# Two attention batches get their transposed queries from the DMA crossbar, and the hand-written step order is set anew

## The chip, the cores and the metric

The kernel runs on one core of a Trainium2 chip. The metric is the device time of one execution in microseconds (us). The kernel before took 223.79 us, the median of 5 runs (223.52 to 224.37).

## What is computed

The program is an attention with 32 memory slots per head, followed by a channel mix over the whole model width. There are 8 batches, 8 heads, 576 tokens per batch, head size 64, model width 512 and inner width 1024.

```python
a = exp(phi - max(phi, axis=2)); a = a / (sum(a, axis=2) + 1e-09)      # over the tokens
k_m = einsum('bhsm,bhsd->bhmd', a, k);  v_m = einsum('bhsm,bhsd->bhmd', a, v)
attn = softmax(scale * q @ k_m^T);  x = attn @ v_m                     # [B, S, H*D] after a transpose
x_prev = x shifted by one token
xk = mu_k * x + (1 - mu_k) * x_prev;  xr = mu_r * x + (1 - mu_r) * x_prev
out = sigmoid(xr @ w_r) * (relu(xk @ w_k) ** 2 @ w_v)
```

## The kernel before, in words

**Two halves, one order.** The channel mix walks over 9 chunks (c0 to c8) of 512 tokens. A chunk is 16 groups of matmuls: eight "key" groups (`key`, L510: four 128x512 matmuls, a ReLU on ScalarE and a square on VectorE), four "gate" groups (`gate`, L526) and four "value" groups (`value`, L543, which ends in a product on VectorE and in stores on SyncE's queue). The attention of a batch is some 30 small steps (`attention`, L234). A step and a chunk group both have a number, their slot: the groups have slots 0 to 143, and a step of batch b has the position in its table plus 16 times (b - 1), or the bare position for batch 0. The program sorts everything by slot and emits it (L562 to L572). So the tables decide in which order each engine gets its instructions; each engine then runs its own list in order, and waits only on data and on buffers. A step whose position is lower stands earlier in the queues of all engines that it uses.

**The tables.** `STEADY` (L18) holds the order for every batch without a table of its own. `FIRST` (L23) has tables for batches 0 to 3 before. Letters behind a `+` are the PSUM buffers that the step takes in turn: `a` is a pool of three banks that only attention uses, `k` the two banks of the key groups, `v` the three banks that gates and values use. Without letters a step takes `a`.

**The steps that matter here.** `exp` (L246) exponentiates phi on ScalarE. `kv`, or `k` and `v` apart (L254), are 40 small matmuls. `z` (L270) is the sum and its reciprocal on VectorE. `nk` (L279) scales k on VectorE, `tk` (L302) transposes it on TensorE and copies it out on VectorE. `q0` to `q3` (L320) transpose the queries: six 96x96 transposes on TensorE and one 128x576 copy on VectorE each. `s0` and `s1` (L331) are the scores and their exponentials on ScalarE; they read all four query pieces between them. `l0` to `l3` (L348) are the denominators with a logarithm on ScalarE, `r..z` and `h..z` (L360) the reciprocals on ScalarE, `w` and `y` (L365) the products on VectorE. For batches 2 to 7, `nv`, `x0` to `x3` (L372), `dd` (L389) and `k0d`, `k2d`, `r0d`, `r2d` (L401) make the values, the shifted difference and the mix. Batches 0 and 1 take another way: `nkx` and `nrx` (L411) put mu into the values (eight VectorE operations), and `mk0` to `mr3` (L428) are the mixed values by matmul, each copied out half by ScalarE, half by VectorE. `mub` (L212) loads mu into `mu_b` by four DMAs on SyncE's queue, `mum` (L226) multiplies it out on VectorE, and `busy` (L205) puts matmuls of zeros on TensorE: 18 in all before.

**Queries and loads.** `load` (L298) of batch b issues the loads of batch b + 2 on GpSimd's queue. Query tiles `qs` and transposed query tiles `qT` have two buffers each, so a batch follows the batch two before it into the same buffer. A step `qx` (`cross_q`, L316) is there but in no table before: it makes the whole `qT` of a batch with one transposing DMA on SyncE's queue:

```python
nc.sync.dma_start_transpose(out=q_tile().rearrange("p h j t -> p (h j) t"),
                            in_=qs[b % 2].rearrange("p h j d -> p (h j d)"))
```

Of the kernel before, what the change touches and what calls it, by code (L numbers as in the profile page):

```python
# [14 lines left out]

STEADY = [("exp", -20), ("q3", -16), ("q2", -15), ("kv+v", -14), ("z+v", -12), ("nk", -12), ("nv", -12),  # L18
          ("q1", -11), ("q0", -11), ("tk+v", -11), ("s1+aa", -8), ("s0+va", -8), ("load", -7),
          ("l1+a", -6), ("l0+k", -6), ("l3+a", -6), ("r0z", -6), ("w0", -4), ("l2+a", -1), ("r1z",  # L20
          0), ("w1", 0), ("x0+av", 2), ("x3+aa", 4), ("x2+vv", 6), ("x1+aa", 6), ("dd", 8), ("r0d",
          9), ("k2d", 12), ("k0d", 13), ("r2d", 22)]
FIRST = {  # L23
    0: [("busy2_748059", -69), ("busy1_148982", -61), ("busy2_192243", -58), ("exp", -58), ("mub", -55),
        ("mu", -51), ("k+a", -50), ("z+v", -50), ("nk", -47), ("busy1_9643", -46), ("mum", -43),
        ("tk+k", -43), ("q0", -42), ("q1+v", -42), ("q3+a", -41), ("q2+v", -35), ("s0+av", -33),
        ("l0+v", -31), ("l1+a", -31), ("s1+va", -25), ("h0z", -25), ("y0", -23), ("h1z", -23),
        ("busy3_339813", -20), ("l2+k", -19), ("l3+v", -18), ("busy3_529042", -18), ("v+v", -15),
        ("y1", -15), ("h2z", -13), ("nkx", -12), ("busy2_337394", -11), ("busy1_474373", -10),
        ("y2", -9), ("h3z", -9), ("load+a", -7), ("y3", -6), ("mk0+kk", -6), ("mk1+a", -6),  # L30
        ("busy1_380911", -5), ("mk2+aa", -5), ("mk3+vv", -3), ("busy1_810794", -2), ("nrx", -2),
        ("mr1+aa", 2), ("mr2+vv", 4), ("busy1_47294", 4), ("mr0+vv", 4), ("mr3+aa", 4)],
    1: [("exp", 5), ("z+v", 7), ("k+a", 8), ("q0+v", 9), ("q2", 9), ("nk", 9), ("q3", 9), ("q1+v", 9),
        ("tk+v", 10), ("s0+aa", 10), ("s1+va", 10), ("l1+a", 11), ("l3", 11), ("l0+v", 11), ("h3z",
        11), ("h0z", 11), ("l2+k", 11), ("h1z", 11), ("v+k", 12), ("nkx", 12), ("nrx", 12), ("y0",
        12), ("y3", 12), ("y1", 12), ("h2z", 14), ("y2", 14), ("mk0+kv", 14), ("mr1+va", 14),
        ("mk3+vv", 14), ("mr3+kk", 14), ("mk2+aa", 14), ("mk1+vv", 15), ("mr0+ka", 15), ("load+a",
        16), ("mr2+av", 17)],
    2: [("exp", -4), ("q0", -1), ("q1+v", -1), ("q3+a", 0), ("z+k", 0), ("kv+v", 0), ("nk", 0), ("tk+v",
        1), ("q2", 1), ("s0+kv", 2), ("s1+va", 2), ("l0+v", 3), ("l1+a", 3), ("load+k", 3), ("r0z",  # L40
        4), ("w0", 5), ("nv", 5), ("l3+a", 5), ("l2+v", 5), ("r1z", 6), ("x0+a", 8), ("w1", 9),
# [4 lines left out]
        ("l3+k", 5), ("r0z", 5), ("w0", 5), ("r1z", 5), ("w1", 6), ("x0+ka", 7), ("x1+va", 7),  # L46
        ("x2+vv", 8), ("x3+kk", 8), ("dd", 9), ("k2d", 9), ("load+k", 9), ("k0d", 11), ("r2d", 13),
        ("r0d", 15)],
}
LOADS = {None: ("phi", "k", "v", "q"), 2: ("phi", "k", "q", "v"), 3: ("phi", "k", "q", "v"), 4: ("phi", "k", "q", "v")}  # L50
ORDER = ('phi', 'k', 'q', 'wv', 'v')
# [11 lines left out]
def kernel(  # L63
# [13 lines left out]
    nc = tc.nc  # L77
# [145 lines left out]
        nc.tensor.transpose(ps_mu, mu2, ident_f)  # L223
        nc.vector.tensor_scalar_add(mu1, ps_mu, -1.0)

    def spread_mu():  # L226

        for w in range(2):
            mask = maskk.rearrange("p h d -> p (h d)").unsqueeze(1).to_broadcast([128, 2, 2 * D])
            nc.vector.tensor_mul(mu_m[:, w, 0], mask, mu_b[:, w])  # L230
            nc.vector.tensor_sub(mu_m[:, w, 1], mask, mu_m[:, w, 0])


    def attention(b):  # L234
        st = {}

        def ps_tile(shape, dtype, name):

            tags = st["tags"]
            tag = {"a": "at", "k": "pk", "v": "pv"}[tags[st["n"] % len(tags)]]  # L240
            st["n"] += 1
            return psum.tile(shape, dtype, name=name, tag=tag, bufs={"at": 3, "pk": 2, "pv": 3}[tag])
        x0 = b * S % RING
# [10 lines left out]
        def ekv(parts):  # L254

            def go():
                w = parts.stop - parts.start
                kvps = ps_tile([128, 2, w, D], F32, "kvps")
                for i in range(w):
                    st["kv"[parts.start + i]] = kvps[:, :, i, :]  # L260
                for j in range(NJ):
                    for h in range(H):
                        c, g = divmod(h, 4)
                        nc.tensor.matmul(kvps[g * M:(g + 1) * M, c], lhsT=em[:, j, h, :],  # L264
                                         rhs=kv5[:, parts, h, j, :],
                                         start=j == 0 and c == 0, stop=j == NB,
                                         skip_group_check=True)
            return go
# [42 lines left out]
        def q_tile():  # L311
            if "qT" not in st:
                st["qT"] = work.tile([128, H, NQ // 2, QR], BF16, name="qT", tag="qT")
            return st["qT"]
# [5 lines left out]
        def tr_q(pr):  # L320
            def go():
                ps = ps_tile([128, 2, NQ // 2, QR], BF16, "qtps")
                for i in range(2):
                    for j in range(NQ // 2):
                        nc.tensor.matmul(ps[:, i, j], rhs=identity[:QR, :QR], is_transpose=True,  # L325
                                         lhsT=qs[b % 2][:, 2 * pr + i, 2 * j:2 * j + 2, :].rearrange("p j d -> p (j d)"),
                                         start=True, stop=True, skip_group_check=True)
                nc.vector.tensor_copy(q_tile()[:, 2 * pr:2 * pr + 2], ps)  # L328
            return go

        def scores(c):  # L331
# [96 lines left out]
        def mixed(w, c, hf):  # L428

            def go():  # L430
# [15 lines left out]
                for jj in range(2):  # L446
# [3 lines left out]

        two = [(0, 0), (0, 1), (1, 0), (1, 1)]
        steps = {"exp": exp_phi, "kv": ekv(slice(0, 2)), "k": ekv(slice(0, 1)), "v": ekv(slice(1, 2)),
                 "z": esum, "nk": norm_k, "nv": norm_v, "tk": tr_k, "load": reload, "mu": load_mu, "mub": load_mu_b, "mum": spread_mu, "qx": cross_q}
        for i in range(4):
            steps[f"q{i}"] = tr_q(i)
            steps[f"l{i}"] = denom(*two[i])
# [106 lines left out]
    for b in range(B):  # L563
        steps = attention(b)
        for n, (name, pos) in enumerate(FIRST[b] if b in FIRST else STEADY):
            todo.append((pos + 16 * (b - 1) if b > 0 else pos, b, n, steps(name)))
# [36 lines left out]
```

## Time and profile before

| | us |
|---|---|
| median of 5 runs | 223.79 |
| the profiled execution, its own time | 224.37 |
| its span, first to last instruction | 222.6 |
| TensorE matmul busy | 206.5 (93%) |
| ScalarE busy | 159.7 (72%) |
| VectorE busy | 142.6 (64%) |
| query transposes on TensorE (192) | 12.4 |
| query copies on VectorE (32) | 13.4 |
| matmuls of zeros (18) | 8.3 |

The time of an execution is longer than the span by what lies before the first and after the last instruction, here 1.77 us. TensorE's busy time counts each matmul from its start to its modelled end, and matmuls overlap: the chain of waits, which counts each stretch of time once, shows what a group really adds. "PEld" is the weight load that precedes a matmul. SyncE's queue ("SPq") carries the stores, and an instruction in it can start only when those ahead of it have been issued.

### The profile page before, as it was taken

To read this page: it belongs to the slowest core of one execution; us is meant where nothing else is said; L and a number is where in the kernel's file an instruction comes from. 1 tells how busy PE (TensorE), PEld (TensorE's weight loads), DVE (VectorE), ACT (ScalarE), POOL (GpSimd) and SP (SyncE) were. 2 spreads that over 40 slices of the span, in tenths; PEclk is the share of its full clock that TensorE was granted. 3 is DMA by queue.
4 is the path that set the end of the run, shared out by engine and by line. 5 is a ranking of instruction groups with operands and counts; after the bars stand their busy time and mean duration, and the time that the engine had idled before them with its cause. 6 is when DMAs were issued, how large, how long until landed. Compare 5 with 4: busy or idle time off the path is not lost.

```text
span 222.6 us, 4576 instructions
## 1 busy us (share of the span) xinstructions
PE 206.5 (93%) x1755; PEld 101.8 (46%) x1755; DVE 142.6 (64%) x356; ACT 159.7 (72%) x309; POOL 47.7 (21%) x66
## 2 busy tenths in 40 slices
PE   4369999899999998999999999999999999999992
PEld 1243345346444564445444864454443444444441
DVE  3162855297565989788867688769875875425322
ACT  2207468983799849997699679967978965765770
POOL 7653351543340639121600000000000000000000
PEclk9999999999999999999999999999999999999998
DMA  6999999999999999999994300330033033033024
GB/s 135 194 200 207 231 204 209 222 222 275 218 238 197 262 202 210 231 197 307 144 187 111 94 3 0 94 97 1 10 98 85 1 94 94 3 94 94 0 65 124
DMA packets 43349, 31.49 MB, mean 141 GB/s; under 512 B 10952, under 2 KB 37840, under 8 KB 43328
## 3 DMA queue, kind: packets, MB, share of 16 engines
q0 software_dynamic: 35248, 20.91, 63.3%
q1 hardware_dynamic: 7776, 9.97, 15.7%
q10 hardware_dynamic: 304, 0.33, 0.4%
q8 instruction: 13, 0.21, 0.4%
q14 instruction: 8, 0.07, 0.1%
HBM read 38.54 MB, written 9.44 MB: 216 GB/s over the span
## 4 chain that ended last, share of the span: by engine, by line
PE 82%; DVE 5%; ACT 4%; DMA 3%; POOL 1%; issue 1%; SPq 1%; DVEq 0%; POOLq 0%
PE pk L518 28%; PE pv L551 27%; PE pr L532 13%; DMA mu_b<-in_moe_mu_r_dram 3%; PE qtps L325 2%; PE kvps L264 2%; PE idle L209 2%; PE nops L382 2%; PE zps L355 2%; PE scps L341 1%; DVE atn L369 1%; PE mxps L439 1%; DVE o L553 1%; ACT e L345 1%; PE zps L274 1%
## 5 line engine op out<-in xcount | busy, mean ns | idle before, releaser
L518 PE MATMUL pk<-xkT,wk 128*128 128x512 bf16 (+1 forms) x320 | 69.4, 358 | 0.0
L551 PE MATMUL pv<-wv,sq 128*128 128x512 bf16 (+1 forms) x296 | 66.2, 373 | 0.0
L522 ACT ACTIVATE rl<-pk 128x512 bf16<-128x512 f32 x72 | 43.1, 601 | 27.0 <-PE pk L518 26.7
L523 DVE TENSOR_TENSOR sq<-rl 128x512 bf16<-128x512 bf16 x72 | 30.4, 422 | 26.0 <-ACT rl L522 25.5
L553 DVE TENSOR_TENSOR o<-sg,pv 128x512 f32<-128x512 f32 (+1 forms) x37 | 24.2, 672 | 31.3 <-ACT sg L540 18.3
L551 PEld LDWEIGHTS <-sq 128*128 128x128 bf16 x296 | 28.6, 98 | 32.0 <-issue 0.4
L518 PEld LDWEIGHTS <-wk 128*128 128x128 bf16 x320 | 29.0, 98 | 26.2 <-issue 1.6
L532 PE MATMUL pr<-wr,xrT 128*128 128x512 bf16 x144 | 35.1, 379 | 0.0
L537 ACT ACTIVATE sg<-pr 128x512 f32<-128x512 f32 x36 | 21.6, 604 | 6.8 <-PE pr L532 6.5
L532 PEld LDWEIGHTS <-xrT 128*128 128x128 bf16 x144 | 13.3, 98 | 15.9 <-issue 1.2
L540 ACT ACTIVATE sg<-sg 128x1024 f32<-128x1024 f32 x18 | 19.0, 1057 | 0.6
L539 ACT ACTIVATE sg<-sg 128x1024 f32<-128x1024 f32 x18 | 19.0, 1057 | 0.6
L345 ACT ACTIVATE e<-scps 128x288 bf16<-128x288 f32 x32 | 10.8, 428 | 9.9 <-PE scps L341 9.9
L407 DVE TENSOR_SCALAR mu_d<-diff,mu 128x576 bf16<-128x576 bf16 x48 | 16.3, 382 | 0.2
L386 ACT CAST x<-nops 128x288 bf16<-128x288 f32 x48 | 16.0, 416 | 0.0
L328 DVE COPY qT<-qtps 128x576 bf16<-128x576 bf16 x32 | 13.4, 448 | 1.3 <-PE qtps L325 1.3
L369 DVE TENSOR_TENSOR atn<-e,lz 128x576 bf16<-128x576 bf16 (+1 forms) x20 | 12.3, 632 | 2.9 <-ACT lz L362 2.5
L325 PE MATMUL qtps<-identity,q 96*128 96x96 bf16 x192 | 12.4, 215 | 0.8 <-DMA q<-in_q_dram 0.8
L325 PEld LDWEIGHTS <-q 96*128 96x128 bf16 x192 | 10.9, 103 | 4.3 <-DMA q<-in_q_dram 1.2
L357 ACT ACTIVATE lz<-zps 128x288 f32<-128x288 f32 x32 | 11.2, 411 | 1.2 <-PE zps L355 1.2
L362 ACT ACTIVATE lz<-lz 128x576 f32<-128x576 f32 (+1 forms) x20 | 11.4, 596 | 0.0
L248 ACT ACTIVATE em<-phm 128x1024 bf16<-128x1024 f32 x8 | 8.4, 1055 | 3.3 <-DMA phm<-in_phi_dram 3.3
(66 smaller groups left out, 188.0 us busy)
## 6 DMA issues: line engine op xcount, KB each, us to landing
out_dram<-o SPq DMA_DIRECT2D x23, 192.0 KB, 2.3
kv<-in_k_dram POOLq DMA_DIRECT2D x8, 512.0 KB, 12.3
q<-in_q_dram POOLq DMA_DIRECT2D x7, 576.0 KB, 15.1
phm<-in_phi_dram POOLq DMA_DIRECT2D x7, 512.0 KB, 13.1
kv<-in_v_dram POOLq DMA_DIRECT2D x7, 512.0 KB, 13.4
out_dram<-o SPq DMA_DIRECT2D x23, 128.0 KB, 2.4
out_dram<-o SPq DMA_DIRECT2D x23, 64.0 KB, 2.0
wk<-in_moe_w_k_dram POOLq DMA_DIRECT2D x2, 512.0 KB, 12.3
```

Source lines behind the costliest of these rows:

```text
L325: nc.tensor.matmul(ps[:, i, j], rhs=identity[:QR, :QR], is_transpose=True, lhsT=qs[b % 2][:, 2 * pr + i, 2 * j:2 * j + 2, :].rearrange("p ...
L386: nc.scalar.copy(st["x"][:, 2 * c + jj, sl], pss[jj])
L407: nc.vector.tensor_scalar_mul(t[:, i], st["d"][:, pr + i, :], mu1[:, o:o + 1])
L518: nc.tensor.matmul(pk[:, lo:hi], lhsT=wk_sb[:, di, fi * 128:(fi + 1) * 128], rhs=xk_T[:, di, c0:c0 + hi - lo], start=(di == 0), stop=(di = ...
L522: nc.scalar.activation(rl, pk, AF.Relu)
L523: nc.vector.tensor_mul(st["sq"][:, fi, :], rl, rl)
L532: nc.tensor.matmul(pr, lhsT=xr_T[:, di, c0:c0 + 128], rhs=wr_sb[:, di, :], start=(di == 0), stop=(di == ND - 1))
L537: nc.scalar.activation(sg[:, ts % 2], pr, AF.Exp, scale=-1.0)
L539: nc.scalar.activation(sg, sg, AF.Ln, bias=1.0)
L540: nc.scalar.activation(sg, sg, AF.Exp, scale=-1.0)
L551: nc.tensor.matmul(pv[:, cols], lhsT=st["sq"][:, fi, ts * 128:(ts + 1) * 128], rhs=wv_sb[:, fi, cols], start=(fi == 0), stop=(fi == NF - 1))
L553: nc.vector.tensor_mul(o[:, cols], st[ts // 2][:, ts % 2, cols], pv[:, cols])
```

## The change

Batches 6 and 7 get tables of their own. In them `q0` to `q3` are gone and one `qx` stands in their place, at slot 59 for batch 6 (position -21) and at slot 88 for batch 7 (position -8); the scores of the two batches stand at slots 71 and 88. `STEADY` is then used by batches 4 and 5 only, and its steps move by up to three slots, with `q1`, `q3` and `x3` on other buffers. The tables of batches 0 and 1 are new: for batch 0 the matmuls of zeros go from 18 to 9, `mum` is cut in two (`mum0` for mu_k, `mum1` for mu_r), `z` goes ahead of `mub` and `k`, and the copies of `q1` and `q3` go from VectorE to ScalarE; for batch 1 the steps `y0` to `nrx` move to slots 12 and 13 and all eight `m` steps to slot 15. Tables 2 and 3 are the same.

```diff
-STEADY = [("exp", -20), ("q3", -16), ("q2", -15), ("kv+v", -14), ("z+v", -12), ("nk", -12), ("nv", -12),
-          ("q1", -11), ("q0", -11), ("tk+v", -11), ("s1+aa", -8), ("s0+va", -8), ("load", -7),
-          ("l1+a", -6), ("l0+k", -6), ("l3+a", -6), ("r0z", -6), ("w0", -4), ("l2+a", -1), ("r1z",
-          0), ("w1", 0), ("x0+av", 2), ("x3+aa", 4), ("x2+vv", 6), ("x1+aa", 6), ("dd", 8), ("r0d",
-          9), ("k2d", 12), ("k0d", 13), ("r2d", 22)]
+STEADY = [("exp", -20), ("q2", -16), ("q3+a", -15), ("kv+v", -14), ("z+v", -12), ("nk", -12), ("nv", -12),
+          ("q0", -11), ("q1+a", -11), ("tk+v", -11), ("s1+aa", -8), ("s0+va", -8), ("load", -6),
+          ("l0+k", -6), ("l1+k", -5), ("l3+a", -5), ("r0z", -5), ("w0", -3), ("l2+a", 1), ("r1z",
+          1), ("w1", 1), ("x3+ak", 4), ("x0+av", 4), ("x2+vv", 6), ("x1+aa", 6), ("dd", 6), ("r0d",
+          8), ("k2d", 11), ("k0d", 13), ("r2d", 22)]
 FIRST = {
-    0: [("busy2_748059", -69), ("busy1_148982", -61), ("busy2_192243", -58), ("exp", -58), ("mub", -55),
-        ("mu", -51), ("k+a", -50), ("z+v", -50), ("nk", -47), ("busy1_9643", -46), ("mum", -43),
-        ("tk+k", -43), ("q0", -42), ("q1+v", -42), ("q3+a", -41), ("q2+v", -35), ("s0+av", -33),
-        ("l0+v", -31), ("l1+a", -31), ("s1+va", -25), ("h0z", -25), ("y0", -23), ("h1z", -23),
-        ("busy3_339813", -20), ("l2+k", -19), ("l3+v", -18), ("busy3_529042", -18), ("v+v", -15),
...
+    0: [("exp", -62), ("z+k", -56), ("busy1_653415", -56), ("mub", -55), ("k+k", -53), ("mu", -48), ("nk",
+        -46), ("tk+v", -44), ("q0+v", -43), ("q1+a", -40), ("q3+a", -40), ("s0+a", -39), ("q2+k",
+        -38), ("l0+a", -35), ("h0z", -35), ("l1+a", -32), ("busy2_658043", -27), ("mum0", -27),
+        ("s1+kv", -25), ("h1z", -25), ("v+v", -24), ("l3+v", -24), ("y0", -24), ("y1", -24),
+        ("l2+v", -22), ("h2z", -22), ("busy2_100606", -20), ("h3z", -19), ("nkx", -15), ("load+a",
+        -8), ("y2", -7), ("y3", -7), ("busy2_335180", -5), ("mk1+a", -5), ("mk0+kk", -5), ("mk2+aa",
+        -4), ("mum1", -3), ("busy1_305423", -2), ("mk3+vv", -1), ("nrx", -1), ("mr2+aa", 2),
+        ("busy1_343727", 3), ("mr0+vv", 3), ("mr1+ka", 4), ("mr3+av", 4)],
-    1: [("exp", 5), ("z+v", 7), ("k+a", 8), ("q0+v", 9), ("q2", 9), ("nk", 9), ("q3", 9), ("q1+v", 9),
-        ("tk+v", 10), ("s0+aa", 10), ("s1+va", 10), ("l1+a", 11), ("l3", 11), ("l0+v", 11), ("h3z",
-        11), ("h0z", 11), ("l2+k", 11), ("h1z", 11), ("v+k", 12), ("nkx", 12), ("nrx", 12), ("y0",
-        12), ("y3", 12), ("y1", 12), ("h2z", 14), ("y2", 14), ("mk0+kv", 14), ("mr1+va", 14),
-        ("mk3+vv", 14), ("mr3+kk", 14), ("mk2+aa", 14), ("mk1+vv", 15), ("mr0+ka", 15), ("load+a",
-        16), ("mr2+av", 17)],
+    1: [("exp", 5), ("z+a", 7), ("k+a", 9), ("q0+v", 9), ("q2+k", 9), ("nk", 9), ("q1+k", 9), ("q3+a", 9),
+        ("tk+v", 9), ("s0+ak", 9), ("s1+va", 9), ("l0+v", 10), ("l1+k", 10), ("l3", 10), ("h0z",
+        10), ("y0", 12), ("l2+a", 13), ("v+k", 13), ("h1z", 13), ("nrx", 13), ("nkx", 13), ("y1",
+        13), ("h2z", 13), ("y2", 13), ("h3z", 13), ("y3", 13), ("mr0+va", 15), ("mk0+kv", 15),
+        ("mr1+ka", 15), ("mk1+vv", 15), ("mr3+kk", 15), ("mk2+aa", 15), ("mk3+vv", 15), ("mr2+av",
+        15), ("load+k", 16)],
...
+    6: [("exp", -23), ("qx", -21), ("kv+v", -15), ("z+v", -12), ("nk", -12), ("nv", -12), ("tk+v", -11),
+        ("load+k", -11), ("s1+va", -9), ("s0+va", -9), ("l1+k", -6), ("l0+k", -5), ("r0z", -5),
+        ("l2+k", -5), ("l3+a", -4), ("w0", -3), ("r1z", 1), ("w1", 1), ("x1+av", 3), ("x0+vv", 5),
+        ("x3+aa", 6), ("x2+vv", 6), ("dd", 7), ("r0d", 7), ("k0d", 12), ("k2d", 13), ("r2d", 19)],
+    7: [("exp", -19), ("z+k", -12), ("kv+a", -12), ("nk", -12), ("tk+v", -11), ("nv", -11), ("qx", -8),
+        ("s0+va", -8), ("s1+ak", -8), ("load+k", -8), ("l1+k", -6), ("l0+k", -6), ("r0z", -5),
+        ("w0", -4), ("l2+a", -4), ("l3+a", -4), ("r1z", -4), ("w1", -4), ("x0+va", -1), ("x3+aa",
+        -1), ("x2+vv", 5), ("x1+av", 5), ("dd", 7), ("r0d", 9), ("k0d", 12), ("k2d", 13), ("r2d",
+        20)],
 }
...
-    def spread_mu():
-
-        for w in range(2):
+    def spread_mu(w):
+
+        def go():
             mask = maskk.rearrange("p h d -> p (h d)").unsqueeze(1).to_broadcast([128, 2, 2 * D])
             nc.vector.tensor_mul(mu_m[:, w, 0], mask, mu_b[:, w])
             nc.vector.tensor_sub(mu_m[:, w, 1], mask, mu_m[:, w, 0])
+        return go
...
-                nc.vector.tensor_copy(q_tile()[:, 2 * pr:2 * pr + 2], ps)
+
+                (nc.scalar.copy if b == 0 and pr % 2 else nc.vector.tensor_copy)(q_tile()[:, 2 * pr:2 * pr + 2], ps)
```

## The prediction on record

> **What bounds the kernel now.** I read the busy row first (PE 93%), then the windows by stage, then the chain of waits, then SyncE's queue and the DMA row. The windows cut the run at its chunks:
>
> ```profile
> core 0: us, PE busy (x) PEld busy (x) DVE busy (x) ACT busy (x) POOL busy (x), PEclk, DMA share, GB/s
> ...
> 42.00:53.00 11.00, 10.53 (x115) 5.29 (x114) 8.04 (x22) 8.24 (x20) 4.90 (x7) 1.00 1.41 226
> ...
> 122.50:144.00 21.50, 21.50 (x217) 13.37 (x216) 16.82 (x40) 18.15 (x37) 0.00 (x0) 1.00 0.18 50
> 144.00:165.50 21.50, 21.50 (x186) 10.31 (x184) 17.51 (x42) 17.21 (x35) 0.00 (x0) 1.00 0.18 51
> ```
>
> In chunks c4 and c5 (122.5 to 165.5) TensorE is never idle, while VectorE and ScalarE have 3 to 5 us to spare per chunk: there a group taken from TensorE is worth what it adds to the chain. For c5 the chain has
>
> ```profile
> 144.04 0.86 PE pk L518 x4
> 144.91 0.26 PE qtps L325 x6
> 145.16 0.87 PE pk L518 x4
> 146.03 0.26 PE qtps L325 x6
> ...
> 151.34 0.51 PE qtps L325 x12
> ```
>
> The 24 query transposes of batch 7 add 0.26 + 0.26 + 0.51 = 1.03 us, and the key groups beside them keep 0.86. Before 53 us it is another picture, the chain runs over other engines:
>
> ```profile
> 8.13 5.99 DMA mu_b<-in_moe_mu_r_dram
> 14.21 0.44 DVE mu_m L230
> 14.67 0.42 DVE mu_m L231
> 15.29 0.38 DVE qT L328
> 15.71 0.84 PE scps L341 x8
> ...
> 44.73 2.07 DVE vm L417 x8
> 46.80 1.10 DVE atn L369 x3
> 47.90 1.21 DVE o L553 x2
> ```
>
> At the start VectorE sits on mu's DMA with the key and query copies behind it; around 45 us VectorE, with `nkx` and `nrx` of batch 1, holds TensorE. Last, SyncE's queue and the DMA row (40 slices of 100 to 160 us):
>
> ```profile
> 145.78 1.11 SPq L499 DMA_DIRECT2D out_dram<-o  x2
> ```
>
> ```profile
> DMA  9999499999967600640000000037204710000000
> ```
>
> The stores of c4 are issued by 146.89, and from 123 us the DMA engines carry little but stores.
>
> **What the Trainium skill says.** "DMA: Bandwidth & Descriptors", "Issuing engines are not separate DMA queues": DMAs of all issuers share the same 16 engines; the row above agrees, and shows them idle where `qx` of batch 7 would run. The same page, "Latency and other measured facts", gives a DMA transpose 261 GB/s; its "Anatomy of one DMA" gives about 2.0 us fixed per DMA (this trace: a store lands 2.3 us after its issue). "VectorE: DVE Perf Modes", "The three transpose paths", prices one 128x128 crossbar transpose at 1309 ns. No transposing DMA is in this trace. "TensorE: Matmul & The Clock Gate", Part 1: the array runs at half rate until about 3.4 us of activity; the trace agrees, zero matmuls step by 0.42 us at 21.9 and key matmuls by 0.216 (2.59 / 12) at 25.35.
>
> **The change part by part.**
>
> *Queries of batches 6 and 7.* Off TensorE: 48 transposes, 2 x 1.03 = 2.06 us, all on the bound. Off VectorE: 8 copies of 448 ns, 3.6 us, worth nothing by themselves, as VectorE isn't late there. Added: two DMAs of 96 x 3072 x 2 B = 590 KB. Price: low end 590 / 261 = 2.3 us with no fixed part; my value 2.3 + 2.0 = 4.3 us (an estimate from the DMA page); high end 24 blocks of 96x128 in a row at 1.309 us = 31 us (an estimate from the DVE page). A gain beyond the 2.06 us is excluded: nothing else waits on these queries. What hides it: batch 6's `qx` stands behind the stores of c3's second value group, issued by 119.27 (117.28 + 1.99); its scores, now after c4's last key group, come at 132.72 - 1.03 = 131.7: 12.4 us of cover. Batch 7's `qx` has slot 88, but SyncE runs ahead to it as soon as c4's stores are issued, 146.89, that is 3.1 us after TensorE ends c4 (143.76). Its scores come 11.25 us after that point before (155.01), and 11.25 - 1.03 - 0.25 (a denominator moved forward) = 10.0 us now: 6.8 us of cover. At 4.3 us both are hidden. Queued behind each `qx` on SyncE are only stores, the next ones 4 us (123.33) and some 11 us later, with three buffers for `o`: no cost. The other waits of `qx` are over: batch 7's queries were issued at 109.08 and landed after 9.2 us, and the `qT` buffer is free since the scores of batch 5 (112).
>
> *Steady steps, batches 4 to 7.* The same instructions in nearly the same places, beside a TensorE without gaps: nothing to gain. `x3+ak` and `z+k` take a key bank, so a key group may wait for a ReLU (0.60 us, with 0.74 us of other TensorE work between); `s1`, `s0` of batch 6 come ahead of a gate that needs their bank, some 0.15 us by the ScalarE times (1.3 us of exponentials). Ends: 0 and 0.6; I take +0.2. The loads move by one slot, but GpSimd waits for buffers (9.0 us of idle on an exponential), not for slots: 0.
>
> *Batch 0.* `mum` leaves the way of the copies. `mub` now follows `z`'s reciprocal, so SyncE issues at about 7.6 instead of 6.13 (nothing else is queued there until the first store at 44.76), and mu_k lands near 14.2, mu_r near 15.6. No step needs them before `nkx`. `s0` is then bound by the second query half (landed 13.70) at 14.2 instead of 15.71; q3's copy on ScalarE (about 0.65) comes ahead of the exponentials. From there: `s1` near 17.0 (17.63 before), `v` near 17.9, once its load is in (GpSimd's wait on it ended at 17.18), instead of 21.15, last logarithms 19.9, `h3z` 20.7, `nkx` 19.5 to 20.6 (before 21.93), `y3` 21.4, the `mk` steps from 20.9 with their VectorE copies (0.45 each) to 23.05, `mum1` 0.85, last copy 24.3. First key group near 24.4 instead of 25.35: -0.95. The 9 zero matmuls that go (9 x 0.43 = 3.9 us at half rate) lie in TensorE's slack; there is work enough from 17.0 on to warm it. If not, the first two key groups (8 matmuls) run at half rate: 8 x (0.43 - 0.216) = +1.7.
>
> *Batch 1.* The `mr` steps of batch 0 lie closer, and `k` and the scores leave the gates: I get the end of the second gate at 34.7 (37.14 before), -2.4. Then it is given back. With `q`, `nk`, `tk`, `s` in one bunch, TensorE waits about 0.7 us for `kbd` and 1.2 us for `kmT` behind the query copies, where a gate stood between before: first value group 6.3 us after the gate against 5.06. And `v+k` comes after the second value group, not the first, so VectorE begins its run later: `nrx`, `nkx` 2.15, three `y` 1.2, two `o` 1.35, seven `m` copies 3.15, in all 7.85 us, from 45.2 to about 53.1. The first key group of c1 waits for the last of these: 53.1 instead of 53.38, -0.3; and `mr2` of batch 1, which stands at 56.3 in c1 before, is already done, -0.25. Taken: -0.55. Ends: the whole -2.4 is kept, or VectorE's run is 2 us longer.
>
> **Sum** against the profiled execution (224.37, its span 222.6 and 1.77 around it): -2.06 + 0.2 - 0.55 = -2.4, so 222.0. That execution lies 0.6 above the median of the runs; against the median, 223.8 - 2.4 = **221.4**.
>
> **Rivals.** (a) *The crossbar is slow and TensorE waits at batch 7's scores: slower.* From 6.8 us on every us of `qx` is a us of time, and beyond 6.8 + 2.4 = 9.2 us the kernel is slower than before. At 12 us: 221.4 + 5.2 = 226.6; beyond 12.4 batch 6 stalls too. For it: one block alone is priced at 1.3 us, and 24 of them can't all be hidden. Against: the same page's block is mostly a DMA's fixed part if 2.0 us is right, and the engines are idle. (b) *Partly late*, 6.8 to 9.2 us: at 8 us 222.6. (c) *The start keeps its lead*, if the value groups' cover is enough for VectorE: 221.4 - 1.85 = 219.5. For it: VectorE idles 4.4 us before 44.04. Against: that idleness ends only with `v+k`, which is later now. (d) *The start loses*: VectorE's run 2 us longer or a cold array, 221.4 + 1.9 = 223.3, no change.
>
> **How the numbers follow.** A measurement of this kernel can tell about 0.3% from no change, 223.12 to 224.46. Forecast 221.4: 0.52. (c) 0.14, (d) 0.10, (b) 0.08, (a) 0.16. Faster: 0.52 + 0.14 + 0.06 of (b) + 0.03 of (d) = 0.75; same: 0.02 + 0.06 = 0.08; slower: 0.16 and 0.01 of (d) = 0.17. The range runs from (c), 219.5, to 224.6, (d) with its cold array at 0.5 us more and the mildest part of (a), and leaves out most of (a), whose high end of 31 us would be far beyond: 6.8 of cover against 31 is 24 us for batch 7 alone.
>
> **What would show it.** In the profile after: 144 query transposes, and no wait of TensorE for a DMA at the scores of batches 6 and 7; from `qx`'s issue to its landing under 6.8 us; c4 and c5 one us shorter each (about 20.5); VectorE's copies of keys and queries near 12 us and the first key group near 24.4; second gate near 34.7, first key group of c1 near 53. It is wrong if the scores of batch 7 wait for the DMA, if the first key matmuls step by 0.43 us, or if c1 begins after 54.

## The result, and the profile after

| | before | after |
|---|---|---|
| median, us | 224.08 (48 runs) | 223.15 (27 runs) |
| ratio, 95% interval | | 0.9942 [0.9927, 0.9956] |
| the profiled execution, its own time | 224.37 | 222.08 |
| its span | 222.6 | 220.3 |
| TensorE matmul busy in it | 206.5 | 202.2 |

The kernel is faster by 0.4 to 0.7%, some 1.3 us by the ratio (the two medians are 0.9 us apart); 221.4 us and 1.1% were forecast. The sign was right, the size half or less. The profiled execution of after, 222.08, is not a typical one. Each execution comes with its granted TensorE clock, the share of its full clock that TensorE was given, averaged over the span. In 9 of 28 executions, the profiled one among them, it was 0.999 or 1.0, and their median is 222.08 (mean 222.14); in the other 19 it was 0.988 to 0.992, and their median is 223.27 (mean 223.09). The groups overlap: four of the 19 took under 222.5 us, two of the 9 over 222.9. None of before, in all comparisons, was below 0.995. A mean of 0.992 over 221 us is what some 3.5 us at half clock make (3.5 x 0.5 / 221 = 0.008). Values of 0.995 to 0.998 are no drop of this kind: in the trace of before, 0.996, the half clock begins at 220.85 us, after the last matmul, which ends at 218.5.

Chunks c4 and c5 of after, from first key matmul to first key matmul (columns as in the forecast's table, the mean granted clock ahead of the DMA share):

```profile
core 0: us, PE busy (x) PEld busy (x) DVE busy (x) ACT busy (x) POOL busy (x), PEclk, DMA share, GB/s
121.74:142.83 21.09, 21.06 (x194) 12.53 (x193) 15.78 (x37) 17.91 (x37) 0.00 (x0) 1.00 0.28 67
142.83:163.75 20.92, 20.92 (x165) 9.35 (x164) 16.14 (x38) 18.54 (x38) 0.00 (x0) 1.00 0.34 80
```

c4 took 21.09 us instead of 21.56, c5 20.92 instead of 21.50: about half a us less each, where the forecast expected one. TensorE has no gap in c5, and the chain shows why it is shorter: no query transposes lie between its key groups.

```profile
142.99 3.45 PE pk L528 x16
146.45 0.23 PE nops L392 x2
146.68 0.97 PE pk L528 x4
147.64 0.23 PE zps L283 x10
```

SyncE's queue in after (start, duration; several stores of one line are drawn together), and the time from issue to landing in the list of DMA issues:

```profile
119.01 3.20 SPq L326 DMA_TRANSPOSE qT<-q  x1
122.68 22.55 SPq L509 DMA_DIRECT2D out_dram<-o  x12
145.39 3.11 SPq L326 DMA_TRANSPOSE qT<-q  x1
```

```profile
qT<-q SPq DMA_TRANSPOSE x2, 5.2
```

The crossbar holds SyncE's queue for 3.1 to 3.2 us and lands 5.2 us after its issue (the median of the two); no wait of TensorE for a DMA is in the trace from 118 to 165 us. The start is another matter. The chain of after around c1:

```profile
38.40 0.26 PE zps L365 x2
38.66 0.03 issue
38.69 15.71 DMA kv<-in_v_dram
54.40 0.04 issue
54.45 0.63 PE kvps L273 x32
```

One piece of 15.7 us is not an engine but a load: batch 2's v, issued at 38.69 and landed at 54.40. `kv` of batch 2 waits for it, and behind `kv` stands all of TensorE's queue. In before the same load went out at 38.70 and landed 13.4 us later, at 52.1, its tail of 64 KB at 52.9; `kv` came at 54.66, with no wait (lines of GpSimd's timeline, of that load's own entry and of TensorE's timeline):

```profile
38.70 0.89 POOL L124 DMA_DIRECT2D kv<-in_v_dram  x1 [4.58 <-PE qtps L325]
DMA to landing us min/median/max: 13.4/13.4/13.4
54.66 0.74 PE L264 MATMUL kvps<-kv,em 128*32 128x128 bf16 x40
```

The lead of after over before, from the first matmul of each chunk in the two TensorE timelines:

| first key matmul of | before | after | lead |
|---|---|---|---|
| c0 | 25.18 | 22.52 | 2.66 |
| c1 | 53.22 | 51.48 | 1.74 |
| `kv` of batch 2 | 54.66 | 54.45 | 0.21 |
| c2 | 75.85 | 75.43 | 0.42 |
| c3 | 100.82 | 100.28 | 0.54 |
| c4 | 122.32 | 121.74 | 0.58 |
| c5 | 143.88 | 142.83 | 1.05 |
| c6 | 165.38 | 163.75 | 1.63 |
| c7 | 183.78 | 181.59 | 2.19 |

### The profile page after: what moved, and what is told of

Its sections match the earlier page's. It is cut to its first block, busy times and chain, and to the rows that moved or that the text cites. A ratio compares the mean times of both kernels' runs of the same rounds, so it can differ in the third digit from the quotient of the medians.

```text
span 220.3 us, 4457 instructions
## 1 busy us (share of the span) xinstructions
PE 202.2 (92%) x1698; PEld 99.4 (45%) x1698; DVE 139.0 (63%) x346; ACT 161.5 (73%) x311; POOL 47.7 (22%) x66
## 4 chain that ended last, share of the span: by engine, by line
PE 79%; DMA 12%; DVE 3%; POOL 2%; ACT 2%; issue 1%; POOLq 0%
PE pk L528 28%; PE pv L561 25%; PE pr L542 14%; DMA kv<-in_v_dram 12%; PE kvps L273 2%; PE nops L392 2%; PE zps L365 2%; PE qtps L334 1%; PE scps L351 1%; DVE qT L338 1%; PE idle L217 1%; PE zps L283 1%; ACT rl L532 1%; PE mxps L449 1%; POOL kv L132 1%
## 5 line engine op out<-in xcount | busy, mean ns | idle before, releaser
L542 PEld LDWEIGHTS <-xrT 128*128 128x128 bf16 x144 | 13.4, 98 | 15.7 <-issue 1.2
L396 ACT CAST x<-nops 128x288 bf16<-128x288 f32 x48 | 15.7, 419 | 0.2 <-PE nops L392 0.2
L379 DVE TENSOR_TENSOR atn<-e,lz 128x576 bf16<-128x576 bf16 (+1 forms) x20 | 12.4, 633 | 2.3 <-ACT lz L372 2.1
L338 DVE COPY qT<-qtps 128x576 bf16<-128x576 bf16 x22 | 9.3, 450 | 3.5 <-PE qtps L334 3.5
L283 PE MATMUL zps<-ones,em 128*128 128x1 bf16 x80 | 3.5, 165 | 7.5 <-ACT em L257 6.4
L132 POOL DMA_DIRECT2D kv<-in_v_dram x9 | 7.8, 868 | 10.3 <-PE zps L365 4.7
```

The costliest lines, as they stand in the source:

```text
L379: nc.vector.tensor_mul(st["at"][:, c, sl], st["e"][:, c, sl], st["lz"][:, c, sl])
L396: nc.scalar.copy(st["x"][:, 2 * c + jj, sl], pss[jj])
L542: nc.tensor.matmul(pr, lhsT=xr_T[:, di, c0:c0 + 128], rhs=wr_sb[:, di, :], start=(di == 0), stop=(di == ND - 1))
```

## The experiments

Theory after these profiles: the crossbar does its work; the new start wins 1.7 us up to c1 and loses most of it to the load of v; and in the idle time before it the array often goes to half clock. Rivals: the forecast's own reason, that VectorE's run holds c1; and that the crossbar gives less than thought.

**The crossbar alone (e1).** The kernel before with two tables more, which are its `STEADY` without `q0` to `q3` and with `qx`:

```diff
 FIRST = {
+    6: [("qx", -21), ("exp", -20), ("kv+v", -14), ("z+v", -12), ...
+    7: [("exp", -20), ("kv+v", -14), ("z+v", -12), ... ("tk+v", -11), ("qx", -8), ("s1+aa", -8), ...
```

> The kernel before with one edit: batches 6 and 7 take the steady table of before without q0 to q3 and with one transposing DMA (slots 59 and 88). Landing theory (the kernel gains from the crossbar alone, since the start is pinned by the landing of batch 2's v): ratio to before near 0.991, about 2.0 us less, as TensorE loses 2 x 1.03 us on its bound and nothing else is touched. Clock theory (a denser TensorE is granted a lower clock and gives back about 1 us): about 1 us less, 0.995. If the DMAs cost TensorE more than was seen, no gain.

Measured: 222.96 us, ratio 0.9933 [0.9907, 0.9959]. In its profile c4 took 21.01 us from first key matmul to first key matmul (21.56 before) and c5 20.93 (21.50): 1.12 us in all, where the transposes that went had 2.06 us of the chain. (The two chunks take 43.06 us together in before and, within 0.01, in all four other traces with its tables for batches 6 and 7: e5, e10, e17, e18.) No granted clock was below 0.997, so the clock theory falls. Where the other half is shows in the chain of c4, before:

```profile
128.94 0.90 PE pk L518 x8
129.84 0.51 PE qtps L325 x12
130.35 0.13 PE ktps L305 x2
130.48 0.87 PE pk L518 x8
```

and with the crossbar alone:

```profile
128.53 0.42 DVE sq L500
128.96 0.09 DVE rz L254
129.05 0.03 issue
129.08 0.36 DVE kbd L260
129.44 0.05 issue
129.48 0.23 PE ktps L282
129.71 0.03 issue
129.74 0.23 PE ktps L282
129.97 0.87 PE pk L495 x8
```

The key group after `tk` starts 0.51 us earlier, which is what the first twelve transposes took (0.26 + 0.26). By these two chains the last twelve gave nothing: they had stood where TensorE must wait anyway, until VectorE has scaled the keys (`rz`, `kbd`). With them gone the wait is bare, and the two key transposes behind it take 0.49 us instead of 0.13.

**The rest without the crossbar (e2).** The kernel after without its tables 6 and 7, so that `STEADY` with `q0` to `q3` serves batches 4 to 7.

```diff
-    6: [("exp", -23), ("qx", -21), ...
-    7: [("exp", -19), ("z+k", -12), ...
```

> The changed kernel with batches 6 and 7 back on its steady table, so all queries are transposed by TensorE again; new start and new steady steps stay. Landing theory: no gain or up to 0.5 us, ratio 0.998 to 1.000; first key group of the second chunk near 51.5, and the wait for v of batch 2 ends near 54.4. VectorE theory (the prediction's: VectorE's run of nrx, nkx, y and copies sets the second chunk): 0.5 us less and no wait on that DMA.

Measured: 225.09 us, ratio 1.0044 [1.0016, 1.0071]: slower than before. c4 and c5 are as long as before (21.54 and 21.46), c6 is 0.8 us longer (19.19 against 18.40) with two waits of TensorE for a ReLU. In 10 of 14 executions the clock was low, the profiled one among them: its key matmuls behind `kv` of batch 2 run at half clock (0.53 granted from 54 to 56 us).

**The start alone (e10).** The kernel before with the new tables 0 and 1 and the code that goes with them, nothing else.

```diff
-    0: [("busy2_748059", -69), ...
-    1: [("exp", 5), ("z+v", 7), ("k+a", 8), ...
+    0: [("exp", -62), ("z+k", -56), ...
+    1: [("exp", 5), ("z+a", 7), ("k+a", 9), ...
```

> The kernel before with the new order of batches 0 and 1 alone (with mum in two parts and two copies on ScalarE); batches 2 to 7 as before, no crossbar. Theory (v of batch 2 lands when it landed before, and the array often falls to half clock in the wait): 1.000 to 1.004, 0 to 0.9 us slower, and granted clocks of 0.993 or less in about two of three executions. Prediction's step (the start is worth -0.55 us): 0.9975, clocks of 0.995 or more. The whole lead kept (-2.4 us): 0.989.

Measured: 224.48 us, ratio 1.0014 [0.9994, 1.0034]. Eleven of 22 executions had a low clock (0.988 to 0.991), median 225.4; the other eleven have a median of 223.81, 0.4 below before. Its timeline of TensorE:

```profile
52.72 0.39 PE L250 MATMUL zps<-ones,em 128*128 128x1 bf16 x10
54.11 1.05 PE L240 MATMUL kvps<-kv,em 128*32 128x128 bf16 x40 [1.00 <-DMA kv<-in_v_dram]
```

So the start is worth some -0.4 us where the clock holds, executions with a low clock are 1.5 us longer, and on the whole it gains nothing.

**The old start under the rest (e6).** The kernel after with the order of batches 0 and 1 of before (`mum0` and `mum1` one behind the other, all query copies on VectorE).

```diff
-    0: [("exp", -62), ("z+k", -56), ...
-    1: [("exp", 5), ("z+a", 7), ("k+a", 9), ...
+    0: [("busy2_748059", -69), ... ("mum0", -43), ("mum1", -43), ...
+    1: [("exp", 5), ("z+v", 7), ("k+a", 8), ...
```

> The changed kernel with the tables of batches 0 and 1 of before (mum0 and mum1 side by side where mum was, all query copies on VectorE), so new steady steps and both crossbar transposes stay. Landing theory with half clock: no wait for v and no half clock, TensorE reaches the second chunk just after the landing, so about as the changed kernel or 0.5 us less, ratio 0.991 to 0.994. If the new start were worth what the prediction took for it (0.55 us), 0.997.

Measured: 221.73 us, ratio 0.9883 [0.9858, 0.9908], no low clock in 6 executions; `kv` of batch 2 came at 53.34 with no wait. With the old start the change does better than with its own (0.9942; 0.9919 in e8, whose interval overlaps). The traces of the start need care: the same order of batches 0 and 1 has its first key matmul at 23.85 here, at 24.76 in e9 and at 25.18 in before. The matmuls of zeros show why. They step by 0.43 us, half rate, up to 19.6 here, up to 21.8 in e9 and up to 22.6 in before, and by 0.216 from then on; the traces' records of the granted clock have it full from 19.75, 21.98 and 22.88. When the clock rises differs from trace to trace, and c0 by and large moves with it. The traces of before and after compared above are near each other in this: 22.88 and 22.38.

**Is it the load? (e4, e5, e11)** Batch 2 takes batch 0's queries, whose buffer it shares, so one load of 590 KB ahead of v is gone; its outputs are other ones. e4 and e11 are the same edit of after, e5 of before.

```diff
             elif what == "q":
-                load_q(b)
+                if b != 2:
+                    load_q(b)
```

> The changed kernel without the load of batch 2's queries (590 KB; batch 2 is computed with the queries of batch 0 left in the buffer). v of batch 2 is then issued and lands some 2.8 us earlier. Landing theory: the wait at the values of batch 2 (1.5 us before 54.45) goes, and the kernel is 1.5 to 2.5 us faster than the changed kernel, ratio to before 0.985 to 0.988. VectorE theory: as the changed kernel, 0.994.

> The kernel before without the load of batch 2's queries (batch 2 is computed with the queries of batch 0). Landing theory: before reaches that point 0.3 us after the landing in its profile, so at most 0.3 us less, ratio 0.998 to 1.000, where the same edit is worth 1.5 us or more to the changed kernel. If the load of DMA engines as such slows the whole first half, this kernel gains as much as the changed one.

> The kernel after without the load of batch 2's queries once more (batch 2 uses the queries of batch 0, so its outputs are not the reference's), for a trace of an undisturbed execution. Theory (the landing of batch 2's v holds c1): 0.981 again; v issued by GpSimd some 3 us or more earlier than 38.7, kv of batch 2 without a wait for a DMA, clock 0.996 or more. Rival (VectorE's run holds c1, as the prediction had it): v earlier, but kv of batch 2 at 53 us or later and a wait of TensorE for VectorE ahead of it.

Measured: e4 220.11 us, 0.9807 [0.9761, 0.9854]; e11 219.78 us, 0.9832 [0.9792, 0.9872]; e5 224.16 us, 0.9988 [0.9971, 1.0005]. The load taken from before brings nothing, from after 2.5 to 3 us. GpSimd's queue in e11:

```profile
33.76 0.88 POOL L132 DMA_DIRECT2D kv<-in_v_dram  x1 [1.73 <-PE qtps L335]
```

and its chain:

```profile
48.41 0.37 DVE xkT L459
48.78 0.36 DVE xrT L459
49.14 0.37 DVE xkT L459
49.52 0.04 issue
49.56 0.26 PE mxps L450
49.82 0.15 PE mxps L454 x3
49.96 0.62 PE qtps L335 x12
50.58 0.86 PE pk L529 x4
51.44 0.26 PE qtps L335 x6
51.70 0.23 PE zps L284 x10
51.93 0.67 PE kvps L274 x40
```

v goes out at 33.76 instead of 38.69 and lands at 50.2, `kv` runs at 51.93 with no wait, and c1 lasts 22.48 us (50.41 to 72.89) instead of 23.95. That is 1.5 of the 2.6 us by which this trace is shorter than that of after; the other 1.1 lie ahead of c1, where the clock was full from 18.0 on (from 22.4 in after). VectorE's copies are in the chain, but only up to 49.5: they are not what holds c1. Two of 6 executions of e4 and one of 4 of e11 had a low clock all the same.

**A later place for the step that waits (e3), and its control (e9).** e3 is after, e9 is e6, each with:

```diff
     2: [...
-        ("kv+v", 0), ("nk", 0), ("tk+v", 1), ("s0+kv", 2), ("s1+va", 2), ("l0+v", 3), ("l1+a", 3), ("r0z", 4), ("nv", 5)
+        ("kv+v", 2), ("nk", 2), ("tk+v", 3), ("s0+kv", 4), ("s1+va", 4), ("l0+v", 5), ("l1+a", 5), ("r0z", 5), ("nv", 6)
```

> The changed kernel with batch 2's kv and nk two slots later (after the third key group of the second chunk), and its tk, s0, s1, l0, l1, r0z and nv one or two slots later. Landing theory: TensorE does two key groups (1.7 us) in the wait for v, so 1.5 us less than the full-clock executions, and the array stays warm: 220.5 to 221.5, ratio 0.984 to 0.988. VectorE theory (the second chunk is set by VectorE's run before it): as the changed kernel, 0.994.

> The kernel after with the old order of batches 0 and 1, and with kv, nk and tk of batch 2 two slots later and its next steps up to one or two later. Theory (the later kv pays only because TensorE waits for batch 2's v after the new start): the old start has no such wait, so nothing is gained, 0.988 within 0.0015 as without the later kv, 221.5 to 222.1. Rival (the later order of batch 2 is simply better, wait or none): as much as after the new start, 1.8 us, 0.980 (about 220). A gain of a third of that would leave it open.

Measured: e3 221.35 us, 0.9855 [0.9831, 0.9878]; e9 223.41 us, 0.997 [0.9958, 0.9982]. TensorE in e3:

```profile
53.96 1.03 PE L497 MATMUL pk<-xkT,wk 128*128 128x512 bf16 x4
54.92 0.74 PE L242 MATMUL kvps<-kv,em 128*32 128x128 bf16 x40
```

Two key groups now stand ahead of `kv`, and it starts with no idle time in front. e9 was expected to be as fast as e6 and lost 2 us to it: with the old start v has landed at 51.7, the later place puts `kv` at 57.04, and c1 lasts 24.0 us instead of 22.6 (another 0.9 us between the two traces lies ahead of c0). The edit pays where there is a wait, and only there. e3 is the fastest version that leaves nothing out; e6's interval overlaps with its own.

**The wait filled with zeros (e7), and after once more (e8).** e7 is after with six matmuls of zeros in the wait; e8 is after, unchanged.

```diff
-    2: [... ("z+k", 0), ("kv+v", 0), ...
+    2: [... ("z+k", 0), ("busy6_1", 0), ("kv+v", 0), ...
```

> The changed kernel with six matmuls of zeros (1.3 us at full clock) in TensorE's queue just ahead of the values of batch 2, in the place of its wait. Half-clock theory: no execution near 0.99, and the median is that of the full-clock executions, 222.0 to 222.4, ratio 0.990; the values of batch 2 still start when v lands, near 54.4. Landing theory alone: as the changed kernel, 0.994.

> The changed kernel itself once more, as the base of this set: ratio to before 0.994. Half-clock theory (TensorE idles 1.5 to 2 us for batch 2's v, and in most executions the array then runs at half clock for some 3.4 us): two in three executions show a granted clock near 0.99 and take about 1.2 us longer than those near 1.00. Landing theory alone: the same times whatever the clock.

Measured: e7 221.89 us, 0.989 [0.9869, 0.9911], no low clock in 6 executions. e8 222.19 us, 0.9919 [0.9891, 0.9946], 6 of 10 low. The zeros leave `kv` where it was, at 54.52, still behind the DMA; they save nothing but the clock, and the time is that of the executions of after that kept theirs (222.08). The profiled execution of e8 (0.992) caught the drop, in windows of 2 us:

```profile
core 0: us, PE busy (x) PEld busy (x) DVE busy (x) ACT busy (x) POOL busy (x), PEclk, DMA share, GB/s
52.00:54.00 2.00, 0.51 (x17) 0.42 (x13) 1.01 (x4) 0.60 (x1) 0.00 (x0) 1.00 1.22 318
54.00:56.00 2.00, 1.39 (x41) 0.91 (x43) 0.39 (x2) 0.00 (x0) 0.90 (x2) 0.75 1.36 253
56.00:58.00 2.00, 1.78 (x12) 1.17 (x12) 0.22 (x1) 0.58 (x1) 1.37 (x3) 0.50 1.55 191
58.00:60.00 2.00, 1.68 (x22) 0.60 (x21) 1.16 (x4) 0.81 (x4) 0.89 (x1) 0.90 1.43 198
```

The column to read is the granted clock, third from the right. TensorE is busy for 0.51 of 2 us, then the clock is 0.75, 0.50 and 0.90: 1.0 + 2.0 + 0.4 = 3.4 us at half. c1 lasts 25.74 us here, 1.8 more than in the profiled execution of after.

**Is there a second place? (e13, e14, e15)** In e4's profiled execution (222.45 us, 0.992) the drop lies elsewhere, while batch 1 goes through its scores; two windows of 4 us, columns as above:

```profile
34.00:38.00 4.00, 2.87 (x42) 1.55 (x40) 2.27 (x7) 3.26 (x6) 0.00 (x0) 0.88 1.37 199
38.00:42.00 4.00, 4.00 (x16) 1.74 (x14) 0.00 (x0) 3.14 (x8) 0.89 (x2) 0.69 1.39 239
```

There `q`, `tk` and `s` stand in one bunch, and TensorE in after waits 0.41 us for `kbd` and 0.69 for `kmT`. e14 is after with zeros in that stretch; e13 has those of e7 too; e15 is e3 with zeros in that stretch.

```diff
-    1: [... ("tk+v", 9), ("s0+ak", 9), ...
+    1: [... ("busy2_1", 9), ("tk+v", 9), ("busy3_2", 9), ("s0+ak", 9), ...
```

> The kernel after with matmuls of zeros in both sparse stretches of the new start: 2 ahead of tk and 3 ahead of s0 of batch 1, and 6 ahead of kv of batch 2. Theory (the array goes to half clock in some executions because TensorE is sparse in these two places): no execution with a granted clock under 0.993; 221.6 to 222.2, 0.990. Rival (the half clock comes from elsewhere, the fewer zeros at the very start for one): two to three of ten executions under 0.993 still.

> The kernel after with zeros in the stretch of batch 1 alone (2 ahead of tk, 3 ahead of s0). Theory A (most drops come in the wait for batch 2's v): about half of the executions still under 0.993, time near that of after, 0.993 to 0.995. Theory B (most come in the stretch of batch 1, and filling it is enough): at most one of ten under 0.993, 222.1, 0.991.

> The kernel after with kv of batch 2 later (as in e3) and zeros in the stretch of batch 1. Theory (both sparse stretches are now gone): no execution under 0.993, 221.1 to 221.5, 0.9865 or a little less. Rival (drops elsewhere): some executions under 0.993, 1.2 to 1.5 us longer.

Measured: e13 222.06 us, 0.99 [0.9879, 0.9922]; e14 222.38 us, 0.9925 [0.9903, 0.9947]; e15 221.6 us, 0.9875 [0.9853, 0.9898]. Executions with a clock under 0.993, over all kernels with the new start:

| the wait for v | the stretch of batch 1 | low / executions |
|---|---|---|
| there (after, e2, e8, e10) | sparse | 46 / 74 |
| shorter, 0.64 us (e16, below) | sparse | 1 / 5 |
| there (e14) | filled | 7 / 22 |
| gone or filled (e3, e4, e7, e11, e12) | sparse | 6 / 27 |
| gone or filled (e13, e15) | filled | 0 / 12 |

("Sparse" is a stretch in which TensorE has little to do.) Each place makes the drop in a part of the executions, and with both filled it was not seen; twelve executions are too few to set that apart from the 6 of 27. e14 fits neither of its theories: filling one place is not enough. The fewer zeros at the very start, the rival, are the same in e13 and e15, so by themselves they are not the reason. Where the drop lies in an execution without a trace is not shown.

The four traces that hold a drop (e2, e4, e8, e18) say more. In the clock's records of all traces, every stretch between two changes is a multiple of 3.413 us: the drops last 3.413 us, twice that in e18, and the full clock before them 17.07 (e4) or 34.13. In the 3.41 us just before the drop TensorE was busy for 1.0 (e18), 1.3 (e8), 1.55 (e2) and 2.28 us (e4). Busy time alone does not decide: e3 has 2.29 us in the same place as e4, and no drop.

**Why v lands later (e16, e17, e18).** It lands at 54.0 to 54.6 in the ten traces with the new start and the load of batch 2's queries, at 51.7 to 52.4 in the four with the old one (before, e1, e6, e9), though it is issued at 38.2 to 38.9 in all of them. What differs is the stores of c0: the first is issued at 42.44 in after and at 44.76 in before, the last is out at 49.9 and 53.7. e16 leaves half of them out of after, e17 out of before (tokens 256 to 511 of batch 0 aren't written), e18 makes the other half twice in before.

```diff
-                    store(o, t0 // 128 + ts, cols)
+                    if c or ts < 2:
+                        store(o, t0 // 128 + ts, cols)
```

```diff
                     store(o, t0 // 128 + ts, cols)
+                    if c == 0 and ts < 2:
+                        store(o, t0 // 128 + ts, cols)
```

> The kernel after without the stores of c0's third and fourth value group (tokens 256 to 511 of batch 0 are computed, but not written). Theory (v of batch 2 lands later in after, 54.4 against 52.1 in before with the same issue, because c0's stores come some 2.3 us earlier and take the DMA engines in front of it): 512 KB fewer at 200 to 260 GB/s are 2 to 2.5 us, v lands at 52 to 52.5, the wait of TensorE for it is under 0.3 us, the time some 1.5 to 2.5 us below after, 0.984 to 0.988, and low clocks become rare (at most 3 of 10). Rival (v is late for another reason): it lands at 54.4 and the wait of 1 to 1.5 us stays.

> The same two groups of stores left out of the kernel before. Theory: v of batch 2 lands 1 to 1.5 us earlier than 52.1 (one of the two groups is issued after v has landed there), nobody was waiting for it: no gain, 0.997 to 1.001.

> The kernel before with the stores of c0's first and second value group made twice (the same data to the same place). Theory: 512 KB more ahead of v of batch 2 make it land 1.5 to 2.5 us later, about 54 to 54.6 for its 512 KB part and up to 55.1 for its tail, so that kv of batch 2 waits up to 0.5 us: 1.000 to 1.004. Rival: v lands at 52.1 as before, no wait, 1.000.

Measured: e16 220.55 us, 0.9827 [0.9801, 0.9852], 1 of 5 low; e17 223.58 us, 0.9967 [0.9951, 0.9983]; e18 230.08 us, 1.0262 [1.0224, 1.03]. TensorE in e16:

```profile
53.48 0.81 PE L273 MATMUL kvps<-kv,em 128*32 128x128 bf16 x40 [0.64 <-DMA kv<-in_v_dram]
```

v lands at 53.5 there, 0.9 us earlier than in after, not the 2 that were expected; in e17 it lands at 52.7, not earlier at all. So the stores are a part of the delay, and the larger part of the 2.3 us stays open. e18 says nothing on it: the program issues each second store only when the first one to the same place has landed, 5.2 to 5.9 us after its issue, so the `o` buffers stayed taken, and TensorE stood still for 3.9 us, while v landed at 52.3. It shows something else: behind that idle time the clock was at half for some 6.8 us of the profiled execution, and low in all 6, with the old start.

**The uncovered sum of batch 6 (e12).** e3 with `z` of batch 6 right behind `kv`.

```diff
-    6: [... ("kv+v", -15), ("z+v", -12), ...
+    6: [... ("kv+v", -15), ("z+v", -14), ...
```

> The kernel after with kv of batch 2 later (as in e3) and, in batch 6's table, z two slots earlier, right behind kv. Theory (of the 24 query transposes of a batch the last 12 stood where TensorE had to wait for the normalised keys anyway, so taking them away uncovers the sum, its reciprocal and kbd on VectorE): with the sum earlier tk of batch 6 finds kbd ready and costs about 0.13 us instead of 0.46; c4 from its first key matmul to that of c5 takes 20.75 us instead of 21.10, and the time is 0.984 of before (0.9855 without it), a difference too small for the times alone. Rival (the missing part was lost to other steps that moved): c4 stays at 21.1 and tk still waits.

Measured: 221.75 us, 0.9897 [0.9864, 0.993], 3 of 6 low. In its timeline of TensorE:

```profile
127.13 1.03 PE L497 MATMUL pk<-xkT,wk 128*128 128x256 bf16 x8 [0.33 <-ACT rl L501]
128.00 0.34 PE L283 MATMUL ktps<-identity,kbd 128*128 128x128 bf16 x2
128.19 1.04 PE L497 MATMUL pk<-xkT,wk 128*128 128x256 bf16 x8
```

A miss. `tk` now adds 0.19 us (128.00 to 128.19), not the 0.32 of e3, so the sum had been late; but the key group ahead of it then waits 0.33 us for a ReLU, and c4 is 21.14 us long, not 20.75. Moving the sum uncovered the next wait.

## Why the forecast was half right

**What bounds, and the crossbar: right.** TensorE without gaps in c4 and c5 was the bound, and `qx` was hidden in both places: over the 14 traces that have it, batch 7's landed 4.7 to 6.5 us after its issue, under the cover of 6.8, and batch 6's 5.1 to 7.0, under 12.4. Rivals (a) and (b) are out. But 4.3 was taken, and every one of them was slower: the 2.0 us fixed in that sum is given by "DMA: Bandwidth & Descriptors", "Anatomy of one DMA", for DMAs that GpSimd issues, and this one is on SyncE's queue. The range from 2.3 to 31 us had been opened by a price of "VectorE: DVE Perf Modes", "The three transpose paths", for one 128x128 block; 24 blocks took 5.2 us together in after, so that price doesn't multiply.

**Its gain: mis-sized.** "48 transposes, 2 x 1.03 = 2.06 us, all on the bound" was 1.1 us in the crossbar-only kernel (e1) and 1.6 in after: 0.47 in c4, where the last twelve transposes had been cover for `kbd`, and 1.14 in c5 and c6 together (39.90 to 38.76). These two must be taken together, because batch 7's own table also moves small steps from c6 into c5: c6 is 0.56 us shorter in after, and not at all in e1. That table has the sum ahead of `kv`, and no wait for `kbd` is left in c5. The chain before counted those transposes as TensorE's time because TensorE did them; it can't show what is late behind them. Asking what is late next, as for every other step, would have found it.

**Steady steps: no cost in the chunks that use them.** +0.2 was taken; c3 is 0.04 us shorter. For batches 6 and 7 the same table costs 0.8 us in c6 (e2), but after doesn't use it there.

**The start: the number held, the reason fell.** "The first key group of c1 waits for the last of these: 53.1 instead of 53.38" is wrong: it came at 51.48. All of the start ran ahead of the forecast, c0 from 22.52 and not 24.4, VectorE's run from 43.99 and not 45.2. That -0.55 appears at c3 all the same (0.54) is luck, for it comes by way of another wait: the forecast asked which engine takes the lead back and never which load does. In before v's tail landed at 52.9, 1.8 us ahead of `kv`; a start that is 1.7 us earlier uses that up even if the load keeps its time, and it came 2.3 us later. e11 and e3 show that this load holds c1 in after. That it comes later was not in the forecast, nor in the theory with which e10 was run.

**The step that failed: the start's term, for want of the clock.** "Taken: -0.55" was the forecast for the start; alone it measured +0.3 us (e10, ratio 1.0014; the interval is -0.1 to +0.8 us). The forecast named the half clock only for the first two key groups of c0, where it did not occur. It had seen the bunch in batch 1 ("TensorE waits about 0.7 us for `kbd` and 1.2 us for `kmT`") and priced the wait, not what the array does in it; the wait for v it had not seen.

From 221.4 to 223.15 there are 1.75 us. Of these, 0.3 is the kernel before, 224.08 here against 223.79; 0.4 is that the executions of after with the clock held stand 2.0 below before (222.08), not 2.4; and 1.1, the largest part, is that 19 of 28 executions have a drop and take 1.2 us more by their medians, 0.95 by their means. That the drop is this loss shows in e7 and e13: with zeros in the sparse stretches, and nothing landing earlier, no execution has a drop and the times are 221.89 and 222.06, those of the executions that kept their clock. Trace against trace, both with the clock held, the forecast's 222.0 met 222.08, but that is luck in part, for terms that were off made up for each other: the crossbar gave 0.45 less than taken, and the steady steps didn't cost their 0.2.

Rival (d), "a cold array", 223.3, is what came, at other places and by another way than VectorE. "TensorE: Matmul & The Clock Gate", Part 1, has the rate fall after an idle window of about 3.4 us, a window that runs freely and doesn't start with the kernel. The multiples of 3.413 us in the clock's records agree with such a window, as does that only a share of the executions is hit; but 3.4 us of idleness were not needed: TensorE was busy for 1.0 to 2.3 us of the 3.41 before each drop.

## What to carry to other kernels

When a stage is made earlier, list the loads that its next steps need with their issue and landing: a load need not come earlier with the steps (v was issued at the same time here) and may even land later; the step that needs it is best put where the data arrives, with other work ahead of it. Work that is taken off the bound counts in full only if nothing was waiting beneath it; look for the operation that the removed work stood in front of. And waits of TensorE of 1 to 2 us may cost as much again in a share of the executions, so read the granted clock of all executions, not only of the profiled one.

## What the runs showed of the hardware

- A transposing DMA of 96x3072 bf16 from SBUF to SBUF held SyncE's queue for 2.9 to 3.3 us and landed 4.7 to 7.0 us after its issue (14 traces; in after 3.1 to 3.2, and 5.0 and 5.3).
- A drop of the granted clock is 3.4 us at half (e2, e4, e8), or twice that (e18). It came in 46 of 74 executions with two sparse stretches, in none of 12 with neither.
- Executions with a drop took 1.2 to 2.3 us more than those without, by the medians (after, e2, e8, e10, e14; for example after 223.27 against 222.08, e14 224.38 against 222.09). By itself, 3.4 us at half costs 1.7 us at most (an estimate, half of 3.4), so not all of the 2.3 in e14 is the drop; the rest is not explained.
- The clock became full at 18.0 to 22.9 us, at different times in traces of the same start, and the first key matmul by and large moved with it (19.75 and 23.85 in e6, 22.88 and 25.18 in before).
- v of batch 2 was issued at 38.2 to 38.9 in every kernel that has the load of q(2), and at 32.9 to 33.8 in the three without it (e4, e5, e11). That GpSimd's queue is paced by earlier loads landing would fit this; it is not shown by itself.
